# Chunk 0's key from half-scaled tokens, one-bank PSUM places and a new written order in an adaLN block with sliding attention and a token mixer

## The chip, the core and the metric

The kernel runs on one core of one Trainium2 chip. The metric is the time of one execution on the device in microseconds (us); before the change the median of three runs is 198.68 us (197.99 to 198.73). The core has five engines that run side by side, each working through its own instructions strictly in order: TensorE (PE, matmuls; PEld is its weight load), VectorE (DVE), ScalarE (ACT), GpSimd (POOL) and SyncE (SP), which here does nothing but issue DMAs. ScalarE also issues a few. Engines wait for each other by semaphores. SBUF is the memory that all engines work in; PSUM takes TensorE's results and has eight banks of 128 partitions by 512 float32.

## What is computed

One block on a sequence of 2048 tokens of width 512. Cut to what matters:

```
mod = silu(c) @ w_mod                      # six rows of 512: sa, ca, ga, sb, cb, gb
h = layernorm(x) * (1 + ca) + sa
q, k, v = h @ wqkv                         # 32 heads of 16
# each token attends to 8 tokens: itself, 2 back, 4 back ... 14 back
attn = softmax(q . k / 4, masked before token 0)
x = x + ga * ((attn @ v) @ wo)
h = layernorm(x) * (1 + cb) + sb
u = gelu(w1.T @ layernorm(h) + b1)         # mixes tokens: 2048 -> 1792 rows of 512
x = x + gb * (w2.T @ u + b2)               # 1792 -> 2048
```

Inputs and output are bfloat16.

## The kernel before

The 2048 tokens are cut into four chunks of 512 (`build_chunk(ch)`), each of four tiles of 128 tokens. A chunk goes through these named steps (the number behind the name is the chunk or the tile):

- `ln1s` takes the statistics of a tile, `rstd1` and `nb1` turn them into factors, and `ln1n` normalizes it into `n_sb`.
- `tr` transposes the chunk on TensorE into PSUM, as two halves `kp` of the width. `hT` evicts it into `hTb`, multiplied by `1 + ca` (`a1col`) and with `sa` (`sacol`) added, both as one value for each partition.
- `qkvq`, `qkvk`, `qkvv` are the matmuls, `evq`, `evk`, `evv` their evictions.
- `qk` multiplies q by eight shifted views of k on VectorE (4096 elements for each partition), `red` sums over the head on TensorE. `max`, `sub`, `exp`, `sum`, `rb`, `smul` are the softmax.
- `vd` are 16 DMAs that spread v into `vD`, shifted; `khalo` and `vhalo` bring the last 16 columns of the chunk before. `a2` and `a2ev` spread the weights, `pv` multiplies on VectorE, `pvacc` sums on TensorE, `oev` evicts.
- `wo` is the output projection, whose weights were multiplied by `ga` (`gmul`). `x1ev` evicts it and adds `x`: on VectorE in the eviction itself, on ScalarE by one more matmul with the identity (`on_pe`). `x1sq`, `rstd2`, `nb2`, `t`, `aff` are the second normalization, `ln3s`, `rstd3`, `nb3`, `h3` the third, which ends in `h3`.

Then the mixer: `mlp1_0` multiplies the first eight tiles of `h3` by blocks of `w1`, and its partial sums are parked in `gT` (`park`); `mlp1_1` does the other eight, `gadd` adds both, `gelu` and `gbm` follow; `mlp2` multiplies by `w2`, with `xb` and `fin` on VectorE and the store `st_out`.

What stands at the start: `c` and the first four tiles of `x` are loaded, then `wmodA` and `wmodB`, the halves (by rows) of `w_mod` for `sa` and `ca` together, 512 KB each, then the weights of k, x's next tiles and the weights of q. The silu of `c` is made from the exponential and logarithm (`silu_exp`, `silu_dve`); `modcols0` and `modcols1` compute `sa` and `ca` as columns with 16 one-column matmuls each, and `modcols_cp` evicts both. `warm0` to `warm4` are matmuls with the identity whose result nobody reads. For chunk 0 the transposes come in two halves of the tokens, but an `hT` eviction takes all 512 tokens of one width block. `build_mod_rows` computes the other four modulation rows (`modrows`, `mrow_ev`), and four DMAs (`bc0` to `bc3`) spread them over the partitions.

The order of all of it is written out: `ORDER` names every step, its engine where there is a choice (`:v` VectorE, `:a` ScalarE, `:g` GpSimd) and its place in PSUM (a number). `_Graph.schedule` checks that what a step needs stands ahead of it; then each engine gets its steps in that order, and one that waits holds up all behind it on its engine, DMA issues on SP included. PSUM is held as four tiles of two banks, and a step takes one of the four places, even where it needs one bank.

All instructions are recorded through one helper, so the profile names line 184 for nearly all, and they are told apart by the tiles they write and read.

Of the kernel before, what the change touches and what calls it, by code (L numbers as in the profile page):

```python
# [13 lines left out]
P = 128  # L14
# [13 lines left out]
consts ld_x00 consts2 ld_c warm0:0 ld_x02 ld_wmodA act_table ld_wmodB ld_w1a ld_x1a cps:1 warm1:2 ld_w1b silu_exp  # L28
ln1s0:v ld_x1b ln1s1:a ld_x2 ld_w0 silu_dve halo0 warm2:3 ln1s2:v rstd1_0_0 ln1s3:v modcols0:0 nb1_0_0:v ln1n0:v
warm3:1 rstd1_0_2 ln1n1:v nb1_0_2:v ln1n2:v modcols1 ln1n3:v tr0_00:2 tr0_10:3 modcols_cp:a tr0_02 tr0_12 hT0_0:a  # L30
warm4:1 hT0_1:v hT0_3:v qkvk0_0:0 hT0_2:v sc_rep ln1s7:v ln1s4:v ln1s9:v ln1s8:v ln1s11:v ln1s10:v qkvk0_1:1 qkvk0_2:3
qkvk0_0b qkvk0_1b ln1s5:a ln1s6:a rstd1_1_0 evk0_1:a nb1_1_0:g qkvq0_1:2 qkvq0_0:1 evk0_2:a evk0_0:a evq0_1:a ln1n7:a
# [5 lines left out]
exp0 qkvk1_2:0 modrows:2 tr2_10:3 sum0 evk1_2:a mrow_ev rb0 qk1_1 qk1_0 qk1_3 smul0 nb1_3_0:v qk1_2 tr2_00:0 qkvv1_0:2
a2_0:1 hT2_0:a hT2_1:a hT2_2:a ln1n12:a a2ev0:a evv1_0:a hT2_3:a ln1n15:a ln1n13:a ln1n14:a pv0_0 pv0_1 qkvv1_2:0
red1_0:1 red1_1 red1_2 red1_3 qkvq2_0:2 tr3_00:3 evv1_2:a evq2_0:a hT3_0:a bc0 khalo2 vd1_030 vd1_120 vd1_020 vd1_021  # L40
vd1_010 vd1_000 vd1_001 vd1_100 vd1_031 vd1_110 vd1_011 vd1_131 vd1_130 vd1_111 vd1_121 vd1_101 pvacc0_0:0 pvacc0_1
qkvk2_0:2 max1 pv0_3 pv0_2 oev0_1:a hT3_2:a sub1 tr3_10:0 qkvv2_0:3 evk2_0:a exp1 sum1 pvacc0_2:2 hT3_1:a rb1 hT3_3:a
gmul3:g gmul0:v gmul2:v gmul1:v qk2_1 smul1 qk2_0 pvacc0_3 qkvv2_2:1 oev0_3:a evv2_0:a evv2_2:a wo1:0 a2_1:2 x1ev1:a
a2ev1:a pv1_0 pv1_1 wo3:3 wo0:1 wo2:0 x1ev3:a x1sq1 x1sq3 x1ev0:a x1ev2:a qkvk2_2:2 pvacc1_0:3 qkvq2_2:1 pvacc1_1
x1sq2 evk2_2:a x1sq0 rstd2_0_0 evq2_2:a pv1_2 nb2_0_0:v pv1_3 t0:v qk2_3 qk2_2 qkvq3_0:0 pvacc1_2:2 pvacc1_3 qkvk3_0:1
t2:a t3:a oev1_1:a evq3_0:a oev1_3:a t1:a wo6:3 wo7:0 wo5:2 evk3_0:a x1ev6:a vhalo2 ld_b1 bc2 ld_w1_0_1 khalo3 bc1
vd2_101 ld_w1_0_2 vd2_000 ld_w1_0_0 vd2_131 vd2_121 vd2_010 vd2_001 vd2_030 vd2_031 ld_w1_0_3 vd2_020 red2_0:1 red2_1
wo4:3 x1sq6 x1ev7:a x1ev5:a x1sq7 x1sq5 x1ev4:a x1sq4 rstd2_1_0 red2_2 red2_3 aff0_0 qk3_1 ln3s0_1:v nb2_1_0:v
ln3s0_3:a max2 ln3s0_0:v ln3s0_2:v qkvv3_2:0 qkvk3_2:2 sub2 t4:a t7:g t6:g t5:g evv3_2:a exp2 rstd3_0_0 evk3_2:a
aff1_0 nb3_0_0:v qkvv3_0:3 biascols:0 sum2 qkvq3_2:2 rb2 h3_3:a evv3_0:a evq3_2:a ln3s1_2:a ln3s1_3:a h3_1:g h3_0:g  # L50
ln3s1_0:v biascols_cp ln3s1_1:v h3_2:v qk3_0 smul2 qk3_2 rstd3_1_0 mlp1_0_30_0:1 mlp1_0_31_0 mlp1_0_10_0:0 mlp1_0_11_0
a2_2:3 red3_0:2 red3_1 a2ev2:a nb3_1_0:v qk3_3 h3_6:a h3_4:a h3_5:a h3_7:v red3_2 mlp1_0_00_0:3 mlp1_0_01_0 red3_3
mlp1_0_00_4 mlp1_0_01_4 mlp1_0_10_4 mlp1_0_11_4 pv2_0 max3 park0_0:a sub3 pvacc2_0:3 vd2_120 vhalo3 ld_w1_0_6 vd2_011
ld_w1_0_4 vd3_030 vd2_110 vd2_021 vd2_100 vd2_130 vd3_001 vd2_111 vd3_031 vd3_000 vd3_011 vd3_110 vd3_020 vd3_010
# [160 lines left out]
def _tt1(n):  # L215
    return 0.08 + n / 960.0
# [764 lines left out]
```

## Time and profile before

| what | value |
|---|---|
| median of three runs | 198.68 us (197.99 to 198.73) |
| span of the profiled execution, first to last instruction | 197.0 us |
| time of the profiled execution beside its span | not listed by itself |
| granted TensorE clock, mean | 0.998 |
| busy: TensorE, VectorE, ScalarE, GpSimd | 190.1, 153.5, 123.4, 18.0 us |
| instructions | 3408 |
| read from HBM, written | 22.03 MB, 2.10 MB |

The span begins with the first instruction of any engine and ends with the last. A row of a timeline has the start and the length in us, the engine, the operation, the tiles written and read (buffer numbers left out), the shape and the count; idle time of the engine just before it stands in brackets, with what ended it. Neighbouring instructions of one kind are drawn together. A row of a table by stage gives the busy us of each engine in a stretch.

### The profile page before, as it was taken

How to read it: one execution, taken by the hardware profiler on the slowest of the kernel's cores; microseconds unless marked ns; L12 is line 12 of the kernel's file. 1: busy time of each engine (PE TensorE's matmuls, PEld its weight loads, DVE VectorE, ACT ScalarE, POOL GpSimd, SP SyncE). 2: the span in 40 equal slices, each digit the busy share in tenths (PEclk: the TensorE clock that was granted, in tenths of full speed). 3: DMA queues.
4: the chain of work that ended last, by engine and by line, in shares of the span. 5: the costliest groups of instructions: out<-in, count | busy, mean ns of one | idle time of the engine just before them, and what ended most of it. 6: DMA issues, size and time to landing. Idle time of an engine off the chain costs nothing.

```text
span 197.0 us, 3408 instructions
## 1 busy us (share of the span) xinstructions
PE 190.1 (97%) x1289; PEld 88.2 (45%) x1289; DVE 153.5 (78%) x198; ACT 123.4 (63%) x242; POOL 18.0 (9%) x46
## 2 busy tenths in 40 slices
PE   7889999999999999999999999999999999999994
PEld 2546545445443435433434444444444444444452
DVE  1699989999999999999999999928776127261463
ACT  5498999999999999993769999917541000000000
POOL 7003040090000004300000011000000000000000
PEclk9999999999999999999999999999999999999999
DMA  6999978507994994693999999990000871720112
GB/s 182 369 312 318 302 195 177 120 14 180 171 196 99 270 201 84 187 289 106 174 206 290 234 295 292 292 273 4 0 0 0 229 200 68 199 81 26 57 53 80
DMA packets 45348, 33.59 MB, mean 171 GB/s; under 512 B 5396, under 2 KB 42772, under 8 KB 45332
## 3 DMA queue, kind: packets, MB, share of 16 engines
q1 hardware_dynamic: 44908, 32.82, 67.2%
q10 hardware_dynamic: 424, 0.56, 1.0%
q8 instruction: 10, 0.16, 0.4%
q14 instruction: 6, 0.05, 0.1%
HBM read 22.03 MB, written 2.10 MB: 122 GB/s over the span
## 4 chain that ended last, share of the span: by engine, by line
PE 64%; DVE 12%; DMA 11%; ACT 5%; SPq 3%; issue 2%; ACTq 0%; DVEq 0%
PE ps L184 64%; DMA vD<-v_c 5%; DMA w_q<-in_A_wqkv_dram 4%; SPq L184 3%; DVE pvb L184 3%; DVE prod L184 3%; DMA vD<-in_w_mod_dram 3%; DVE st L184 2%; ACT n_sb L184 1%; DVE h L184 1%; ACT hTb L184 1%; DVE gT L184 1%; ACT v_c L184 1%; DVE ee L184 1%; DVE nm L184 1%
## 5 line engine op out<-in xcount | busy, mean ns | idle before, releaser
L184 DVE TENSOR_TENSOR pvb<-a2sb,vD 128x4096 bf16<-128x4096 bf16 x16 | 36.0, 2284 | 0.2 <-issue 0.2
L184 PE MATMUL ps<-h,wst 128*128 128x512 bf16 x128 | 29.5, 379 | 0.0
L184 DVE TENSOR_TENSOR prod<-q_sb,k_c 128x4096 bf16<-128x4096 bf16 x9 | 20.4, 2285 | 0.1
L184 PEld LDWEIGHTS <-wst 128*128 128x128 bf16 x128 | 12.1, 98 | 16.0 <-issue 1.7
L184 PE MATMUL ps<-gT,vD 128*128 128x512 bf16 x84 | 19.1, 379 | 0.0
L184 PE MATMUL ps<-hTb,w_q 128*128 128x512 bf16 x64 | 15.1, 381 | 1.0 <-DMA w_q<-in_A_wqkv_dram 0.7
L184 DVE TENSOR_TENSOR q_sb<-ps,q_sb 128x512 bf16<-128x512 f32 x8 | 5.4, 687 | 13.6 <-PE ps L184 13.6
L184 PE MATMUL ps<-woq,o_sb 128*128 128x512 bf16 x64 | 15.8, 379 | 0.0
L184 PEld LDWEIGHTS <-w_q 128*128 128x128 bf16 x96 | 9.9, 109 | 12.6 <-issue 2.5
L184 PE MATMUL ps<-hTb,w_v 128*128 128x512 bf16 x64 | 15.0, 380 | 0.0
L184 PE MATMUL ps<-hTb,w_k 128*128 128x512 bf16 x64 | 15.0, 380 | 0.0
L184 DVE TENSOR_TENSOR k_c<-ps,k_c 128x512 bf16<-128x512 f32 (+2 forms) x9 | 5.6, 629 | 11.7 <-PE ps L184 11.7
L184 PEld LDWEIGHTS <-o_sb 128*128 128x128 bf16 x106 | 9.7, 98 | 10.5 <-issue 0.4
L184 PEld LDWEIGHTS <-vD 128*128 128x128 bf16 x116 | 9.2, 97 | 11.4 <-DMA vD<-in_w_mod_dram 1.5
L184 PE MATMUL ps<-gT,pvb 128*128 128x512 bf16 x56 | 12.9, 379 | 0.0
L184 PEld LDWEIGHTS <-w_k 128*128 128x128 bf16 x80 | 8.7, 111 | 8.9 <-issue 0.8
L184 PE MATMUL ps<-gT,prod 128*128 128x512 bf16 x56 | 12.2, 379 | 0.0
L184 PEld LDWEIGHTS <-w_v 128*128 128x128 bf16 x80 | 8.3, 111 | 8.2 <-issue 1.3
L184 ACT ACTIVATE junk<-xx,su 128x512 bf16<-128x512 bf16 x16 | 11.5, 720 | 0.5 <-DVE xx L184 0.2
L184 DVE BATCH_NORM_STATS2 st<-xx 128x6 f32<-128x512 bf16 x11 | 7.4, 671 | 4.7 <-DMA xx<-in_A_x_dram 4.7
L184 ACT ACTIVATE hTb<-ps,sacol,a1col 128x512 bf16<-128x512 bf16 x13 | 9.6, 782 | 0.5 <-PE ps L184 0.5
L184 DVE TENSOR_TENSOR gT<-q_sb,k_c 128x4096 bf16<-128x4096 bf16 x4 | 9.1, 2284 | 0.0
(113 smaller groups left out, 315.1 us busy)
## 6 DMA issues: line engine op xcount, KB each, us to landing
vD<-v_c SPq DMA_DIRECT2D x64, 131.5 KB, 4.6
wst<-in_B_w_dram SPq DMA_DIRECT2D x8, 512.0 KB, 6.1
vD<-in_B_w_dram SPq DMA_DIRECT2D x3, 896.0 KB, 7.3
wst<-in_w_mod_dram SPq DMA_DIRECT2D x4, 512.0 KB, 9.3
prod<-in_B_w_dram SPq DMA_DIRECT2D x2, 896.0 KB, 11.0
pvb<-in_B_w_dram SPq DMA_DIRECT2D x2, 896.0 KB, 8.1
xx<-in_A_x_dram SPq DMA_DIRECT2D x4, 256.0 KB, 4.7
xx<-in_A_x_dram SPq DMA_DIRECT2D x2, 512.0 KB, 7.7
```

Source lines behind the costliest of these rows:

```text
L184: r = fn(*a, **k)
```

## The change

- **Loads at the start.** The first two tiles of `x` come as two DMAs of 128 KB (`ld_x00`, `ld_x01`). Of the two modulation blocks the scale (`ca`) comes first, as two DMAs of 256 KB (`ld_ca0` on ScalarE's queue, `ld_ca1` on SP's), then both halves of k's weights, and only then the shift (`ld_sa`, 512 KB). The weights of q come ahead of `x2`.
- **Column sums.** `colsa` computes the scale's columns over all of the depth in 16 matmuls, `a1_cp` evicts it; `colss` does the shift's, and `sa_cp` evicts it twice, as float32 and as bfloat16 (`sabf`).
- **Chunk 0's key.** The transposed tokens are evicted in halves of 256 tokens (`hk0_0` to `hk3_2`, eight steps), multiplied by the scale alone, into four unused rows of `gT`. The key is computed from these, 32 matmuls of 256 columns (`qkvk0_j_0`, `qkvk0_j_2`) in place of 16 of 512. What the shift adds to the key is one value for each row of k: `kbias` computes it with 16 one-column matmuls of k's weights and `sabf`, and `evk0` adds it as the bias at the eviction, in four steps of one bank each. `hadd0` to `hadd3` add the shift to the scaled tokens for chunk 0's q and v.
- **PSUM.** There are eight places of one bank. A step that needs two banks takes two neighbouring places; transposes, the one-bank parts of chunk 0, `wo`, `mlp2` and the small sums take one. The tiles remain four of two banks. Chunk 0's key holds four places at once. `biascols` writes both of its results into one bank.
- **Order.** `ORDER` is new throughout. On GpSimd there are now `ln1n1`, 5, 4, 11, 8, 10, 9, 13 and 14, all four `gmul`, `t3`, 1, 2, 0, 6, 4 and 15, `h3_1`, 2, 9, 8 and 13, and five of the `nb` steps (before: `ln1n6`, 4, 10, 11, 8, `gmul3`, `t7`, 6, 5, `h3_1`, 0, 8 and two `nb`). `x1ev` is on ScalarE for 14 of 16 tiles (before 9). `bc0` is issued ahead of three of chunk 0's `vd` DMAs.

The core of the diff:

```diff
-consts ld_x00 consts2 ld_c warm0:0 ld_x02 ld_wmodA act_table ld_wmodB ld_w1a ld_x1a cps:1 warm1:2 ld_w1b silu_exp
...
+consts ld_c ld_x00 ld_x01 ld_ca0 ld_ca1 ld_x02 act_table ln1s1:v ld_wk0 ln1s0:a warm4:0 ld_wk2 rstd1_0_0 consts2
+warm0:0 cps:0 silu_exp warm1:1 silu_dve nb1_0_0:v ln1n0:v warm2:1 ln1s2:v ln1s3:a ld_sa colsa:0 rstd1_0_2 ln1n1:g
+warm3:1 halo0 a1_cp:v tr0_10:1 hk1_0:v nb1_0_2:v tr0_00:0 ln1n2:v ln1n3:v hk3_0:v ld_x1b hk0_0:a hk2_0:a ld_x1a tr0_02
+ld_wq tr0_12 ld_b1 hk1_2:v hk0_2:a ld_x2 qkvk0_2_0:2 colss:3 ld_b2 hk3_2:v hk2_2:a ld_wv sa_cp:a hadd3:a ln1s4:a ld_x3
+ln1s7:v qkvk0_0_0:4 qkvk0_3_0:5 qkvk0_1_0:3 kbias:0 qkvk0_0_2 ln1s6:v hadd2:v ln1s5:v ld_wo2 hadd0:a hadd1:v qkvk0_1_2
+qkvk0_3_2 qkvk0_2_2 qkvq0_1:1 qkvq0_2:6 rstd1_1_0 kb_cp:v sc_rep evk0_3:v nb1_1_0:v qkvq0_0:0 ln1n6:v ln1n7:v ln1s10:v
...
+qkvq1_0:2 qkvk1_0:0 red0_0:4 red0_1 red0_2 ld_wmod2 ld_wo1 red0_3 evv0_2:a rstd1_2_0 evq1_0:a ln1s15:a evk1_0:a
+ln1s14:a ln1s12:a ln1s13:v khalo1 vd0_101 qkvq1_2:6 vd0_131 vd0_030 vd0_011 max0 ld_wo3 nb1_2_0:g vd0_031 ln1n11:g
+sub0 ln1n8:g vd0_000 vd0_111 ld_wo0 vd0_021 exp0 vd0_010 ln1n10:g rstd1_3_0 evq1_2:a ln1n9:g qkvk1_2:2 sum0 tr2_10:0
+nb1_3_0:g rb0 tr2_00:1 evk1_2:a hT2_1:a modrows:6 qkvv1_2:4 mrow_ev hT2_3:a hT2_0:a qk1_1 vd0_100 vd0_110 vd0_130
+vd0_020 hT2_2:a bc0 gmul2:g vd0_001 gmul0:g qk1_0 smul0 a2_0:2 qk1_2 qk1_3 qkvv1_0:6 gmul1:g qkvk2_0:0 a2ev0:a
+evv1_0:a gmul3:g red1_0:2 vd0_120 vhalo1 vd0_121 ld_w1_0_0 ln1n13:g ln1n14:g evv1_2:a pv0_0 evk2_0:a ln1n12:a khalo2
...
-    NPS = 4
-    ps = [psp.tile([P, 2, 512], F32, name=f"ps{i}") for i in range(NPS)]
+    NPS = 8
+    ps = [psp.tile([P, 2, 512], F32, name=f"ps{i}") for i in range(NPS // 2)]
...
     def bank(s_, h):
-        return ps[s_.i][:, h, :]
+        return ps[s_.i // 2][:, s_.i % 2 + h, :]
...
+    def f_kb():
+        for j in range(4):
+            for kt in range(KT):
+                nc.tensor.matmul(bank(sl_kb, 0)[:, j:j + 1], lhsT=_ap(w_p[1][:, kt, j:j + 1], [[4, P]]),
+                                 rhs=sabf[:, kt:kt + 1], start=(kt == 0), stop=(kt == KT - 1), skip_group_check=True)
...
+                if ch == 0:
+                    dst = hraw[:, kt, t0:t1]
+                    alts = [("act", _act(n_, 1), lambda dst=dst, src=src, sc_=sc_: nc.scalar.activation(
+                                dst, src(), ACT.Identity, scale=sc_)),
+                            ("dve", 0.32, lambda dst=dst, src=src, sc_=sc_: nc.vector.tensor_scalar(
+                                dst, src(), sc_, None, op0=ALU.mult))]
...
+            for (g0, g1) in parts:
+                for j in range(4):
+                    def f(j=j, g0=g0, g1=g1):
+                        for kt in range(KT):
+                            nc.tensor.matmul(bank(sk[j], 0)[:, g0 * P:g1 * P], lhsT=_ap(w_p[1][:, kt, j:j + 1], [[4, P]]),
+                                             rhs=hraw[:, kt, g0 * P:g1 * P], start=(kt == 0), stop=(kt == KT - 1))
```

More of the change, by code (lines that the diff above doesn't have):

```diff
@@ L27 @@
 ORDER = """
-consts ld_x00 consts2 ld_c warm0:0 ld_x02 ld_wmodA act_table ld_wmodB ld_w1a ld_x1a cps:1 warm1:2 ld_w1b silu_exp
[L29 to L32, printed above, removed]
@@ L38 @@
[L38 to L42, printed above, removed]
@@ new lines, with f_sa_dve @@
+    mod_cols(1, range(KT), "colsa")
+    G.add_any([("act", 0.2, lambda: nc.scalar.activation(a1col[:], bank(sl_m[1], 0)[:, 0:KT], ACT.Identity, bias=1.0)),
+               ("dve", 0.1, lambda: nc.vector.tensor_scalar(a1col[:], bank(sl_m[1], 0)[:, 0:KT], 1.0, None, op0=ALU.add))],
+              reads=[sl_m[1]], writes=["a1col"], name="a1_cp", lat=0.1, use=[sl_m[1]])
+    mod_cols(0, range(KT), "colss")
+    def f_sa_dve():
+        nc.vector.tensor_copy(sabf[:], bank(sl_m[0], 0)[:, 0:KT])
+        nc.vector.tensor_copy(sacol[:], bank(sl_m[0], 0)[:, 0:KT])
```

282 lines of the change are left out of this document (161 added, 121 removed).

## The prediction

> **What bounds the kernel now.** I read the page's busy times first, then the chain that ended last in order of time, then the timeline of each engine over the opening, and last the rows of VectorE and GpSimd side by side.
>
> ```profile
> PE 190.1 (97%) x1289; PEld 88.2 (45%) x1289; DVE 153.5 (78%) x198; ACT 123.4 (63%) x242; POOL 18.0 (9%) x46
> ```
>
> From the chain of waits, three columns: start, us, what:
>
> ```profile
> 1.38 5.32 DMA vD<-in_w_mod_dram
> ...
> 6.71 7.94 DMA w_q<-in_A_wqkv_dram
> ...
> 14.70 19.33 PE ps L184 x145
> ...
> 86.30 106.59 PE ps L184 x585
> ```
>
> TensorE looks full, but a matmul's modelled end overlaps the next one, so small waits hide in "busy". The timeline of TensorE tells more:
>
> ```profile
> 1.41 1.89 PE L184 MATMUL ps<-ident 128*128 128x512 bf16 x4 [1.41 <-POOL onecol L184]
> ...
> 8.23 0.54 PE L184 MATMUL ps<-sc,vD 128*128 128x1 bf16 x16
> 8.64 1.05 PE L184 MATMUL ps<-ident,n_sb 128*128 128x128 bf16 x16
> ...
> 10.40 3.61 PE L184 MATMUL ps<-hTb,w_k 128*128 128x512 bf16 x16
> 14.70 3.65 PE L184 MATMUL ps<-hTb,w_q 128*128 128x512 bf16 x16 [0.69 <-DMA w_q<-in_A_wqkv_dram]
> ...
> 36.58 0.42 PE L184 MATMUL ps<-ee,selB 64*32 64x128 bf16 x32 [0.39 <-DVE ee L184]
> ...
> 192.71 1.38 PE L184 MATMUL ps<-gT,o_sb 128*128 128x512 bf16 x16
> ```
>
> Sixteen matmuls of 512 columns take 3.61, and one alone 0.38 (the groups' mean is 379 to 381 ns): the step from one to the next is (3.61 - 0.38)/15 = 0.2155. After 10.40 the code issues 785 such units: 192 for q, k and v, 64 for `wo` and 9 identity matmuls beside them, 224 each for `mlp1` and `mlp2`, 8 for `sub`, and 64 for `red` and `pvacc` (four quarter-width ones run as one). 785 x 0.2155 = 169.2. Transposes and `sum` (80 at 0.056), `a2` (4 x 0.35) and `modrows` (16 of quarter width, 0.9) add 6.8: 176.0. From 10.40 to the last end, 192.71 + 1.38 = 194.1, pass 183.7, so TensorE loses 7.7 us in waits. The span is 10.4 + 176.0 + 7.7 + 2.9 (last eviction, store) = 197.0.
>
> Where the 7.7 go, a table by stage says (the stretch and its length, then busy us of TensorE, its weight loads, VectorE, ScalarE and GpSimd, the granted clock, the DMA share, GB/s):
>
> ```profile
> 30.00:50.00 20.00, 19.52 (x213) 10.36 (x212) 20.00 (x15) 19.32 (x31) 5.25 (x1) 1.00 0.54 121
> 50.00:70.00 20.00, 19.99 (x156) 8.63 (x155) 19.97 (x13) 19.84 (x40) 0.00 (x0) 1.00 0.90 187
> 70.00:86.30 16.30, 15.62 (x137) 7.28 (x130) 16.09 (x25) 15.95 (x40) 3.78 (x5) 1.00 0.78 177
> ```
>
> From 30 to 86 VectorE has no time left (56.06 of 56.30), and TensorE is fed at its pace; after 86.3 TensorE alone counts. So three things set the time: when q starts, what VectorE has to carry until 86, and TensorE's own work behind that.
>
> **The opening.** The change needs 0.5 MB of modulation weights before the first eviction where before 1 MB was awaited; the two waits named above for `vD` and `w_q` are what it aims at. I follow the new order by the old rows.
>
> ```profile
> 1.78 0.47 SPq L184 DMA_DIRECT2D vD<-in_w_mod_dram  x1
> 1.83 1.28 ACT L184 ACT_TABLE_LOAD   x1 [1.83 <-issue]
> 4.00 0.61 ACT L184 ACTIVATE junk<-xx 128x512 bf16<-128x512 bf16 x1
> 5.46 0.46 ACT L184 ACTIVATE lv<-mv,epscol 128x1 f32<-128x1 f32 x2
> 5.95 0.20 ACT L184 ACTIVATE rs<-lv 128x2 f32<-128x2 f32 x1
> 9.81 1.45 DVE L184 TENSOR_SCALAR hTb<-ps,a1col,sacol 128x512 bf16<-128x512 bf16 x3 [1.10 <-PE ps L184]
> 11.30 0.69 DVE L184 BATCH_NORM_STATS2 st<-xx 128x6 f32<-128x512 bf16 x1
> 16.67 4.49 DVE L184 TENSOR_TENSOR prod<-q_sb,k_c 128x4096 bf16<-128x4096 bf16 x2
> ```
>
> In the rows above, the table load ends at 3.1, so ScalarE takes `ln1s0` from 3.15 to 4.6 (1.46 by the rows 4.00 to 5.46), `rstd1_0_0` to 5.3 (0.69) and `silu_exp`, now behind both, to 5.95. Both column sums and the normalized tiles wait for that: GpSimd has `ln1n1` by 7.1. But TensorE comes later: its first eight warming matmuls stand ahead of `cps`, at some 0.43 each (row 1.41: four in 1.89, less the overlap of the last, an estimate), to 4.8; then eight more at 0.2155, `colsa` and five more, with the wait for the weights between, to 8.2. The transposes run from 8.2. `hk1_0` follows half a microsecond behind the first of them (before: the last transpose at 8.64 + 15 x 0.055 = 9.47, its eviction at 9.81), VectorE does `ln1n2` and `ln1n3` ahead of `hk3_0`, which ends at 10.0. `tr0_02` and `tr0_12` stand in front of the first key matmul and need the halves' readers out of the bank: first key matmul at 10.4, as before.
>
> The key block is the same 32 x 256 columns, 3.5 us (no row has such a matmul; the ends are the 0.055 of a 128-column transpose and a full step's 0.2155, and I take half a step, 0.108, as a quarter of the columns went at a quarter of it with a new load each), and now holds `colss` and `kbias`, 32 one-column matmuls at 25 ns (row 8.23), 0.8. So q can start at 14.8. `hadd0` on ScalarE, behind `sa_cp`, `hadd3` and `ln1s4`, ends at 14.65 by the same sums. Before, q started at 14.70, held by its weights. In the new order the q weights have `x2` behind them instead of ahead (0.5 MB less in their queue), and I take them as landed. Splitting `ld_x00` costs one more SP issue, some 0.47, ahead of `x02`, hidden behind `ln1s0`. For the opening I take **+0.2**, between -0.9 (if the warming matmuls don't hold up the transposes) and +1.0 (a key block at a full step would be +3.4, which the transposes' row speaks against; +1.0 comes if the `hk` or `hadd` steps slip by a stats step, some 0.8: row 11.30 and its short second step). VectorE's first product moves from 16.67 to some 17.6: it takes `evk0_3`, `hadd` and three stats first, but has one stats step fewer between the products and `max0`.
>
> **The move of work.** Fourteen, not nine, `x1ev` evictions are on ScalarE; each brings one identity matmul (`on_pe`), all five added ones behind 86: 5 x 0.2155 = **+1.1** on TensorE, which has no gap there. VectorE's list from its first product to `qk3_3` is shorter by 0.3 (three `gmul`, `t0` and small ones go, three `h3` and `t5` come), and ScalarE's gets four norms fewer. All of that goes to GpSimd, from 11 normalizations and one `gmul` to 21 and four. This is what the sum hangs on, so the rows of GpSimd beside VectorE's:
>
> ```profile
> 14.28 0.20 POOL L184 TENSOR_TENSOR nb<-mv,rs 128x4 f32<-128x4 f32 x1 [9.34 <-ACT rs L184]
> 14.58 0.23 POOL L184 TENSOR_SCALAR nb<-nb 128x4 f32<-128x4 f32 x1
> 25.90 2.27 POOL L184 TENSOR_SCALAR n_sb<-xx,rs,nb 128x512 bf16<-128x512 bf16 x3 [9.48 <-DVE nb L184]
> 38.97 5.25 POOL L184 TENSOR_TENSOR woq<-woq,ga_bc 128x512 bf16<-128x512 bf16 x1 [10.80 <-DMA ga_bc<-mrow]
> 117.95 0.77 POOL L184 TENSOR_SCALAR h<-h,rs,nb 128x512 bf16<-128x512 bf16 x1
> ```
>
> ```profile
> 38.72 4.49 DVE L184 TENSOR_TENSOR pvb<-a2sb,vD 128x4096 bf16<-128x4096 bf16 x2
> 43.13 1.22 DVE L184 TENSOR_REDUCE nm<-ps 128x128 bf16<-128x1024 f32 x1
> 118.19 0.99 DVE L184 TENSOR_SCALAR h<-h,mv,rs 128x512 bf16<-128x512 bf16 x2
> ...
> 120.11 0.73 DVE L184 TENSOR_SCALAR h<-xx,rs,nb 128x512 bf16<-128x512 bf16 x2
> ```
>
> The one `gmul` on GpSimd took 5.25 us: it lay beside two products of VectorE and ended at 44.22, 1.09 after the second gave way to a reduction out of PSUM. And at 118.19 two normalizations of VectorE took 0.99 where the same pair took 0.73 at 120.11 (0.26 lost) while GpSimd held out to 118.72. The two engines exclude each other; the normalizations at 25.90 took 0.76 each because VectorE was at stats and a reduction. The Trainium skill, page "SBUF — State Buffer", section "Who interferes with whom", states this: a VectorE instruction with two SBUF inputs and a GpSimd one that reads SBUF share a port pair, and the one that starts first blocks the other for the whole instruction. By that rule GpSimd would have got in between the two products, at 40.92; the trace says it did not, so I count port time and leave open who waits.
>
> From 27 to 86 the new order gives GpSimd 14 normalizations (0.76), four `gmul` (1.09) and four `nb` pairs (0.6, from 14.28 until the next step at 14.9): 17.4 us. VectorE leaves it free in six stats steps (0.8), three reductions (1.1, row 43.13 less its overlap) and about 1 us of waits: 9.1. So 8.3 us must be taken from products or waited out. Who pays: `tr2` on TensorE needs `ln1n8` to `ln1n11`, `tr3` needs `ln1n13` and `ln1n14` (which stand behind all four `gmul`, and these behind `bc0`), `aff0` needs `t0` to `t3`; behind each stands all of TensorE's or VectorE's queue. Least is nothing, most all 8.3. The nearest row is 118.19, where a normalization of 0.77 cost VectorE 0.26, a third: a third of 8.3 is 2.8, and I take **+2.8**.
>
> `bc0` also moves on SP's queue ahead of the last `vd0` copies, so `pv0_1` waits for `modrows` and `mrow_ev`. I put that inside the ends of the term above: while VectorE waits for them the port is free.
>
> **Banks and order.** Eight one-bank places where four two-bank ones stood let transposes, `wo` and `mlp2` hold half as much, and `mlp1_0` pieces stand earlier in the new order to fill TensorE's waits. The most that can be won is the 7.7. The waits the profile names for TensorE in the middle, 0.39, 0.31 and 0.37, sum to 1.1; I take **-1.0**, ends 0 and -5. The tail is the same by the rows (14 and the last 128 columns of 15 last, their stores behind): 0. `biascols`, two copies, the `hk` evictions (eight of half size for four): under `ln1s` work, 0; without that cover 0.3 each.
>
> **Sum.** +0.2 + 1.1 + 2.8 - 1.0 = +3.1 on a span of 197.0: 200.1. The profile gives the profiled execution's span alone; the middle of the runs, 198.68, is 1.7 above it. So 201.8.
>
> **The rivals.** *Faster:* the places and fillers win back most of TensorE's waits (-5), and GpSimd's work falls into VectorE's free stretches. +0.2 + 1.1 - 5 = -3.7: 195.0. For it: before, GpSimd's eleven normalizations all found such stretches. It decides once the fillers win more than 1.3 plus what the port costs. *Slower still:* VectorE's strings of products keep the port as at 38.97. Then two of `ln1n8` to `ln1n11` pass before `max0` ends at 29.5, and the last waits for `qk1_1` and `qk1_0` (2.2 each, to 34) or also for `smul0`, `qk1_2` and `qk1_3` (to 39.8); TensorE, done with `sum0` at 33, stands at `tr2` for 2 to 7 us. It stands again at `tr3`, where VectorE's `smul1` in turn needs `sum1` from behind `tr3`. That is the whole 8.3 in place of 2.8: 207.3. *Nothing:* the port costs nothing that matters, and the order wins the 1.1 back: 198.9. *A release after each product:* a GpSimd step waits 2.2 at most, and VectorE then pays the whole 0.76 for each of eight steps that fall on products: 6.1 in place of 2.8, 205.1. The row at 38.97 speaks against it. It is the reading of the Trainium skill's page "SBUF — State Buffer", same section.
>
> **How the numbers follow.** Forecast (200 to 204) 0.42; slower still 0.18; a release after each product 0.05; nothing 0.10; faster 0.25. A measurement here can't tell less than 0.5%, 1 us, from no change. Faster 0.25, same 0.10, slower 0.65. The range leaves out a tenth on each side: 195.0 to 206.5; the likeliest case alone has 200 to 204.
>
> **What would show it.** First key matmul at 10.4 and first q at 14.8 (within 0.6). GpSimd steps of over 1.5 us beside VectorE products, or products of over 2.5; a wait of TensorE at `tr2` or `tr3` named GpSimd or `n_sb`. Five more identity matmuls on `xx`. It is wrong if q starts before 14, or if GpSimd's normalizations stay at 0.77 and products at 2.28 throughout, or if TensorE's losses after 10.4 fall under 6.

## The result and the profile after

| | before | after |
|---|---|---|
| median | 198.68 us (197.99 to 200.11, 5 runs) | 229.83 us (228.70 to 233.38, 5 runs) |
| ratio | 1 | 1.154, 95% interval 1.147 to 1.161 |
| forecast | | 201.8, range 195.0 to 206.5 |

The change costs some 30 us where 3 were forecast. Two of the five runs after, the profiled one of 232.47 us among them, lie over 1.5% above the fastest, so the ratio above and the differences below go by the other three, whose median is 229.0 us, and the rows are read for where time is lost, not for the total.

From the page, the busy times:

```profile
PE 200.4 (87%) x1326; PEld 93.2 (40%) x1326; DVE 153.9 (67%) x189; ACT 125.4 (54%) x257; POOL 45.7 (20%) x65
```

VectorE and ScalarE do what they did before (153.9 and 125.4 against 153.5 and 123.4), but TensorE now covers 87% of its span instead of 97%, and it is busy 10 us longer with nearly the same matmuls. The waits are visible in the timeline of TensorE (start, length, then in brackets how long it stood idle just before and what ended that):

```profile
6.28 1.86 PE L188 MATMUL ps<-ident 128*128 128x512 bf16 x4 [1.16 <-ACT ecol L188]
8.47 1.86 PE L188 MATMUL ps<-ident 128*128 128x512 bf16 x4 [0.33 <-DVE sc L188]
...
13.93 0.38 PE L188 MATMUL ps<-ident,n_sb 128*128 128x128 bf16 x4 [0.44 <-DVE gT L188]
15.70 0.69 PE L188 MATMUL ps<-ident,n_sb 128*128 128x128 bf16 x8 [1.39 <-ACT gT L188]
16.19 1.06 PE L188 MATMUL ps<-gT,w_k 128*128 128x256 bf16 x4
...
22.06 2.10 PE L188 MATMUL ps<-hTb,w_q 128*128 128x512 bf16 x9
...
63.36 0.29 PE L188 MATMUL ps<-ident,n_sb 128*128 128x128 bf16 x1 [6.29 <-POOL n_sb L188]
```

The first key matmul starts at 16.19 (before 10.40), q at 22.06 (before 14.70). The strange rows are the first two. `warm1` and `warm2` multiply the identity by itself, read nothing that was computed, and yet wait for `ecol`, the silu of `c`, and for `sc`. VectorE's side of the same stretch:

```profile
8.25 0.16 DVE L188 TENSOR_TENSOR sc<-ps,ecol 128x4 bf16<-128x4 f32 x1 [2.65 <-PE ps L188]
...
12.89 0.16 DVE L188 TENSOR_SCALAR a1col<-ps 128x4 f32<-128x4 f32 x1 [3.26 <-PE ps L188]
...
23.12 0.16 DVE L188 COPY kbcol<-ps 128x4 f32<-128x4 f32 x1 [2.46 <-PE ps L188]
```

`sc` reads place 0, whose one matmul ended at 5.1, and `ecol`, which is ready by 6.7; it waits until 8.25, when `warm1` in place 1 is done. `a1col` reads place 0 and waits for `warm3` in place 1; `kbcol` reads place 0 and waits for q's block in place 1. In each pair the two places are the two banks of one PSUM tile. The change cut the places in half but left the tiles at two banks, and the program's waits go by tile.

The second loss is GpSimd's. From its timeline and from VectorE's:

```profile
49.88 10.64 POOL L188 TENSOR_TENSOR woq<-woq,ga_bc 128x512 bf16<-128x512 bf16 x4 [5.54 <-DMA vD<-v_c]
60.50 3.56 POOL L188 TENSOR_SCALAR n_sb<-xx,rs,nb 128x512 bf16<-128x512 bf16 x2
```

```profile
49.79 5.45 DVE L188 TENSOR_TENSOR pvb<-a2sb,vD 128x4096 bf16<-128x4096 bf16 x2
55.16 1.21 DVE L188 TENSOR_REDUCE nm<-ps 128x128 bf16<-128x1024 f32 x1
56.29 6.37 DVE L188 TENSOR_TENSOR pvb<-a2sb,vD 128x4096 bf16<-128x4096 bf16 x2
```

Four scalings took 10.64 us, and the pairs of products beside them 5.45 and 6.37 where such a pair took 4.49 before. `ln1n13` and `ln1n14` stand behind the scalings, and `tr3` on TensorE waits 6.29 us for them (the last TensorE row above).

A third loss is TensorE's clock. Two rows of a table by stage (stretch and length, busy us of TensorE, its weight loads, VectorE, ScalarE and GpSimd, granted clock, DMA share, GB/s):

```profile
10.00:20.00 10.00, 7.91 (x77) 5.19 (x76) 4.29 (x13) 3.81 (x12) 0.00 (x0) 0.83 1.11 326
60.00:70.00 10.00, 6.17 (x33) 3.09 (x34) 3.58 (x3) 2.31 (x5) 4.06 (x3) 0.66 0.92 156
```

In finer stretches the clock is at 0.50 from 16.1 to 19.5, nearly all of the first half of the key block, and from 60.5 to 67.3, and at 1.00 elsewhere before the last matmul. TensorE works for some 6.9 us of these; at half the clock that is by estimate 3.4 us lost. Before the change the clock stays at 1.00 until the last matmul.

### The profile page after: what moved, and what is told of

Read it like the earlier page. It is cut to its first block, busy times and chain, and to the rows that moved or that the text cites. A ratio compares the mean times of both kernels' runs of the same rounds, so it can differ in the third digit from the quotient of the medians.

```text
span 230.8 us, 3508 instructions
## 1 busy us (share of the span) xinstructions
PE 200.4 (87%) x1326; PEld 93.2 (40%) x1326; DVE 153.9 (67%) x189; ACT 125.4 (54%) x257; POOL 45.7 (20%) x65
## 4 chain that ended last, share of the span: by engine, by line
PE 49%; ACT 28%; DVE 8%; POOL 6%; issue 4%; DMA 3%; SPq 0%; DVEq 0%; ACTq 0%
PE ps L188 49%; ACT junk L188 9%; POOL woq L188 3%; ACT xx L188 3%; DVE h L188 3%; ACT v_c L188 3%; ACT q_sb L188 2%; ACT lv L188 2%; ACT hTb L188 2%; DVE q_sb L188 2%; DVE st L188 2%; ACT o_sb L188 2%; POOL n_sb L188 2%; DMA xx<-in_A_x_dram 1%; ACT k_c L188 1%
## 5 line engine op out<-in xcount | busy, mean ns | idle before, releaser
L188 DVE TENSOR_TENSOR pvb<-a2sb,vD 128x4096 bf16<-128x4096 bf16 x16 | 38.7, 2462 | 3.5 <-PE ps L188 2.2
L188 PE MATMUL ps<-woq,o_sb 128*128 128x512 bf16 x64 | 16.3, 379 | 3.3 <-ACT xx L188 2.3
L188 POOL TENSOR_SCALAR n_sb<-xx,rs,nb 128x512 bf16<-128x512 bf16 x9 | 13.3, 1490 | 18.7 <-DVE nb L188 14.8
L188 PE MATMUL ps<-hTb,w_v 128*128 128x512 bf16 x64 | 16.5, 404 | 0.2 <-ACT q_sb L188 0.2
L188 PE MATMUL ps<-ident,n_sb 128*128 128x128 bf16 x64 | 5.7, 230 | 10.6 <-POOL n_sb L188 7.8
L188 PEld LDWEIGHTS <-w_k 128*128 128x128 bf16 x112 | 11.3, 116 | 8.2 <-issue 1.2
L188 POOL TENSOR_SCALAR h<-h,rs,nb 128x512 bf16<-128x512 bf16 x5 | 4.7, 946 | 48.8 <-DVE nb L188 48.8
L188 PEld LDWEIGHTS <-ident 128*128 128x128 bf16 (+1 forms) x77 | 7.1, 108 | 13.9 <-issue 9.2
L188 ACT ACTIVATE hTb<-ps,sacol,a1col 128x512 bf16<-128x512 bf16 x12 | 8.9, 784 | 6.4 <-PE ps L188 6.4
```

The source lines that it names most:

```text
L188: r = fn(*a, **k)
```

## The experiments

The theories: **A**, neighbouring places of one PSUM tile wait for each other; **B** (B1 in its sharper form), GpSimd and VectorE keep each other out (the port of the prediction), and strings of products make it dear; **C**, a rival of both: the new loads and the new order are late by themselves. D, E and F came up on the way and are explained where they appear. All ratios are against the kernel before on the same chip.

**apart.** Only place numbers differ from the changed kernel, 86 of them, beginning so:

```diff
-warm1:1 warm2:1 colsa:0 warm3:1 tr0_10:1 colss:3 qkvk0_0_0:4 qkvk0_3_0:5 qkvk0_1_0:3 kbias:0
+warm1:2 warm2:2 colsa:2 warm3:4 tr0_10:4 colss:6 qkvk0_0_0:3 qkvk0_3_0:4 qkvk0_1_0:0 kbias:5
```

> The changed kernel with its order, engines and loads untouched; only place numbers differ, so that one-bank steps that are alive together stand in different two-bank tiles where there is room (12 waits between neighbours of one tile are left in the program, of 39). Theory A (neighbours in one tile wait for each other): the first key matmul starts at 10.4 to 12 us instead of 16.19, q at 15 to 18 instead of 22.06, the whole 7 to 14 us shorter than the changed kernel, 214 to 222. Theory B (the shared port of GpSimd and VectorE is the whole loss): the opening moves but the end stays above 226. Rival C (the new loads and the new order themselves are late): first key matmul stays at 15 to 16 us, total 227 to 231.

222.72 us (ratio 1.124, 1.121 to 1.126): 6.3 shorter than the changed kernel's 229.0 (6.0 by the two ratios), a little less than the 7 to 14 that A said. Its TensorE timeline:

```profile
10.73 0.60 PE L188 MATMUL ps<-gT,w_k 128*128 128x256 bf16 x4
...
15.17 3.62 PE L188 MATMUL ps<-hTb,w_q 128*128 128x512 bf16 x16
...
55.02 0.29 PE L188 MATMUL ps<-ident,n_sb 128*128 128x128 bf16 x1 [6.28 <-POOL n_sb L188]
...
56.38 3.62 PE L188 MATMUL ps<-hTb,w_v 128*128 128x512 bf16 x8
...
60.65 1.92 PE L188 MATMUL ps<-hTb,w_v 128*128 128x512 bf16 x8
```

The key starts at 10.73 and q at 15.17, nearly as before the change: C is wrong for the opening's start. The GpSimd wait of 6.28 stays, and behind it eight matmuls take 3.62 that take 1.92 four microseconds later: here the clock is at 0.50 from 50.4 to 60.7 (see apart_gm_warm).

**before_pairs.** The same theory from the other side: the kernel before with nothing changed but how PSUM is declared.

```diff
-    ps = [psp.tile([P, 2, 512], F32, name=f"ps{i}") for i in range(NPS)]
+    quad = [psp.tile([P, 4, 512], F32, name=f"ps{i}") for i in range(NPS // 2)]
+    ps = [quad[i // 2][:, 2 * (i % 2):2 * (i % 2) + 2, :] for i in range(NPS)]
```

> The kernel before, its order, places and engines untouched; only the PSUM tiles are declared twice as large, so that places 0 and 1 lie in one tile of four banks and places 2 and 3 in another. No address, instruction or order differs. Theory A: steps in neighbouring places now wait for each other, the time rises by 10 to 50 us, to 209 to 250, and new waits of VectorE and ScalarE on PE named ps appear. If waits go by bank and not by tile: 198 to 200, no change.

274.97 us (1.384, 1.374 to 1.394): 76 us for a declaration, more than A's 50. From its table of waits (us in total, times, longest):

```profile
PE ps L184 <- ACT ee L184: 10.3, 3, 8.1
PE ps L184 <- ACT a2sb L184: 8.2, 4, 3.9
DVE xx L184 <- PE ps L184: 8.5, 2, 6.5
```

TensorE waits for evictions it has nothing to do with, and VectorE for matmuls whose result it does not read. The chip does not ask for this, since the kernel before runs the same instructions in 198.5 us without these waits; the program does. The Trainium skill, page "PSUM — Partial Sum Buffer", section "PSUM bank collisions raise a hardware error", asks to guard PSUM by bank and quadrant, two readers included; by that rule no two banks need a wait, and here the waits go wider than it. No run here shows what happens on one bank without a wait.

**pool_back and apart_pool_back.** Sixteen steps that the change had put on GpSimd go back, in the new order (but the three scalings stand later in it), once with the changed kernel's places and once with those of apart.

```diff
-ln1n5:g nb1_2_0:g ln1n9:g nb1_3_0:g gmul2:g gmul0:g gmul1:g ln1n13:g ln1n14:g nb2_0_0:g t3:g t1:g t2:g t0:g nb2_1_0:g t4:g
+ln1n5:v nb1_2_0:v ln1n9:a nb1_3_0:v ln1n13:a ln1n14:a gmul2:v gmul0:v gmul1:v nb2_0_0:v t3:a t1:a t2:a t0:v nb2_1_0:v t4:a
```

> The changed kernel with 16 steps that it had moved to GpSimd put back on the engines they had before (three scalings of the output weights, four of the norms n_sb, five of the t norms, four of the small means); places as in the changed kernel. Theory B: the idle TensorE before tr2 and tr3 that is named after n_sb of GpSimd (8.0 us together) falls under 2, the n_sb steps take 0.8 us each or under 1.5, pairs of pvb products take 4.5 to 4.7 us instead of 5.45 and 6.37; total 8 to 14 us shorter, 214 to 220. Theory A as the whole loss: within 2 us of the changed kernel, 226 to 231.

> Both edits. If A and B are both right and add up: 200 to 210. If they overlap (one only uncovers the other): no better than the better of the two alone by more than 3 us. If C is right: above 222.

233.99 us (1.178, 1.173 to 1.184) and 222.16 (1.121, 1.116 to 1.126): pool_back is some 5 longer than the changed kernel, apart_pool_back no shorter than apart. Taken alone that speaks against B, but the waits of apart_pool_back show that the edit brought its own:

```profile
DVE nb L188 <- ACT rs L188: 17.0, 7, 7.7
...
PE ps L188 <- DVE nm L188: 5.1, 1, 5.1
```

The waits for `n_sb` ahead of `tr3` are gone, as B said, but the small means `nb2`, now on VectorE at the place where GpSimd had them, make VectorE stand 7.7 us for ScalarE's `rs`, and TensorE then stands for `nm`. The edit took out one wait and put in another. So the next one leaves the second half of the list where it is.

**apart_gm, apart_gm_max, apart_gm_max_x1.** On top of apart: only the three scalings (again later in the order) and four norms of the first layer go back; then also `max2` ahead of the steps that wait for GpSimd's t norms (theory **D**: the place of that reduction costs TensorE 3.8 us); then also five `x1ev` back on VectorE.

```diff
-ln1n5:g ln1n9:g gmul2:g gmul0:g gmul1:g ln1n13:g ln1n14:g
+ln1n5:v ln1n9:a ln1n13:a ln1n14:a gmul2:v gmul0:v gmul1:v
-aff0_0 red2_2 ln3s0_2:v red2_3 qkvv3_0 ln3s0_3:v qk3_1 ln3s0_0:v max2 ln3s0_1:a
+red2_2 red2_3 max2 aff0_0 ln3s0_2:v ln3s0_3:v ln3s0_0:v ln3s0_1:a qkvv3_0 qk3_1
-x1ev9:a x1ev10:a x1ev11:a x1ev14:a x1ev15:a
+x1ev9:v x1ev10:v x1ev11:v x1ev14:v x1ev15:v
```

> The kernel apart with three scalings of the output weights, ln1n5 and the norms ln1n9, ln1n13 and ln1n14 back on VectorE and ScalarE; the t norms and small means stay on GpSimd, other than in pool_back. Theory B1 (strings of VectorE products keep GpSimd out, and tr3 pays for it): the 6.3 us in which TensorE waits for n_sb ahead of tr3 and the slow matmuls behind it go, the first matmul with the output weights starts at 57 to 59 us instead of 66.0; total 212 to 215 against 222.7. If apart_pool_back showed no gain because GpSimd's work costs nothing: 221 to 224.

> apart_gm with chunk 2's max (VectorE) moved in the order ahead of chunk 0's affine step and its statistics and of the product qk3_1, no engine changed. Theory D (the new order puts VectorE's reduction behind steps that wait for GpSimd's t norms, and TensorE waits 3.8 us for nm at 88 to 92): that wait falls under 1 us, total 3 to 7 us below apart_gm, 206 to 211. If the place in the order does not matter: within 1 us of apart_gm.

> apart_gm_max with the evictions x1ev 9, 10, 11, 14 and 15 back on VectorE, so five identity matmuls fewer. By the prediction's term 0.4 to 1.1 us shorter than apart_gm_max; if ScalarE's queue between 120 and 150 us is what holds TensorE there, 2 to 4 us shorter; if VectorE is the fuller engine there, longer.

apart_gm took 216.35 us (1.089, 1.083 to 1.095), 6.4 below apart, somewhat less than B said. The other two took 217.28 (1.093, 1.083 to 1.103) and 218.11 (1.096, 1.088 to 1.104): D falls, and the five identity matmuls of the prediction cannot be seen. Why D falls is one row of TensorE in each. First apart_gm, then apart_gm_max:

```profile
85.35 1.01 PE L188 MATMUL ps<-nm,ident 128*128 128x512 bf16 x2 [4.19 <-DVE nm L188]
```

```profile
86.48 3.57 PE L188 MATMUL ps<-hTb,w_k 128*128 128x512 bf16 x8 [4.88 <-ACT v_c L188]
```

With the reduction moved ahead, `nm` is in time, and now ScalarE's eviction `v_c` is late, since a statistics step that waits for `aff0` stands ahead of it on ScalarE. At this place both engines have steps in line behind one chain (t norms on GpSimd, `aff0` on VectorE), and TensorE is out of other work. Moving one step only changes the name of the wait.

**before_gmul.** B in the kernel before, alone:

```diff
-gmul0:v gmul2:v gmul1:v
+gmul0:g gmul2:g gmul1:g
```

> The kernel before with the three scalings of the output weights moved from VectorE to GpSimd, behind the one that is there already; nothing else differs. Theory B1: the four scalings run from 39.0 to 52 to 56 us (3 to 5 us each beside the products), and the first matmul with the output weights waits for the last: 52.5 to 56 instead of 51.69; total 199.5 to 204. If the port does not matter: four scalings of 1.0 us, 197 to 199.

200.25 us (1.008, 1.005 to 1.012): by the ratio 1.7 longer, inside what B1 said. The group of scalings on GpSimd (ns: shortest, median, longest; start of first and last):

```profile
L184 POOL TENSOR_TENSOR woq<-woq,ga_bc x4: 1150/3204/3971, 43.4 to 51.6; 128x512 bf16<-128x512 bf16 x4
```

The one that falls on VectorE's reduction takes 1.15, the median beside products 3.2. No engine is named as waiting for the scalings; what grows is VectorE's pair of products beside them, 6.40 us in place of 4.49.

**open_only and open_places.** The changed kernel's opening, 89 steps, and behind it the kernel before: its order, engines and places. (open_only also has chunk 0's statistics and norms on the old engines.) The two kernels differ in eleven place numbers of the opening, those of apart and those of the changed kernel:

```diff
-warm1:2 warm2:2 colsa:2 warm3:4 tr0_10:4 colss:6 qkvk0_0_0:3 qkvk0_3_0:4 qkvk0_1_0:0 kbias:5 qkvq0_0:4
+warm1:1 warm2:1 colsa:0 warm3:1 tr0_10:1 colss:3 qkvk0_0_0:4 qkvk0_3_0:5 qkvk0_1_0:3 kbias:0 qkvq0_0:0
```

> The changed kernel's opening (its first 89 steps: scale block first, key from scaled tokens in halves, shift as bias) with the places of apart, and behind it the order, engines and places of the kernel before (each place there as a tile of its own). Theory E (what is left after the false waits and the port is the new order behind the opening): 197 to 201, TensorE's first key matmul 10 to 11 us, q at 14.7 to 15.5. If the opening itself, its loads or its longer bias path costs: 203 to 212. If the opening gains: below 197.

> open_only with one difference: the opening's place numbers are those of the changed kernel, so 15 waits between neighbouring places are in the program instead of 3. Theory A: first key matmul at 15 to 16.5 us and q at 20.5 to 22.5 as in the changed kernel, and the time 5 to 8 us above open_only. If the late loads and not the places made the changed kernel's opening late: same as open_only within 1 us.

202.00 us (1.021, 1.018 to 1.024) and 208.82 (1.057, 1.052 to 1.061): the eleven numbers alone cost 6.8, as A said. open_only itself is above what E said, and its q is late. TensorE in open_only, then in open_places:

```profile
11.08 0.60 PE L188 MATMUL ps<-gT,w_k 128*128 128x256 bf16 x4
...
16.81 3.61 PE L188 MATMUL ps<-hTb,w_q 128*128 128x512 bf16 x16 [1.14 <-ACT hTb L188]
```

```profile
6.99 1.86 PE L188 MATMUL ps<-ident 128*128 128x512 bf16 x4 [1.87 <-ACT ecol L188]
...
14.98 0.61 PE L188 MATMUL ps<-ident,n_sb 128*128 128x128 bf16 x8 [1.39 <-ACT gT L188]
...
22.06 2.10 PE L188 MATMUL ps<-hTb,w_q 128*128 128x512 bf16 x9 [1.55 <-ACT hTb L188]
```

The same waits as in the changed kernel come back with the numbers, and q is at 22.06 to the hundredth.

**open_only2, open_eng, apart_eng.** open_only2 has chunk 0's steps on the changed kernel's engines; with it the order and the places of the opening are the same in all four cells of a table of order against engines (57 steps have other engines; six of them, `ln1s4` to `ln1s6`, `ln1n6`, `ln1n7` and `nb1_1_0`, belong to chunk 1 but stand inside the opening). The order brings its places with it: by the expectations' counts the new one still has 12 waits between neighbours of one tile, the opening alone 3. Theory **E**: the order carries what is left.

```diff
-ln1s1:a ln1s0:v ln1s3:v ln1n1:v
+ln1s1:v ln1s0:a ln1s3:a ln1n1:g
```

> The changed kernel's opening, now with chunk 0's own statistics and norms on the engines of the changed kernel (open_only had put them back), places apart, and behind it order, engines and places of the kernel before. Theory E (the opening alone costs next to nothing, the order behind it and its engines cost the rest): q at 15.0 to 15.6, 198.5 to 201. If the opening costs by itself as in open_only: 201.5 to 203.

> open_only2 with the 57 steps behind the opening put on the engines of the changed kernel, their places in the old order kept. If the engines carry the rest (GpSimd's added work and the longer way of the t norms): 212 to 222. If the new order carries it: 200 to 206.

> The other cell: apart with the same 57 steps on the engines of the kernel before, in the new order (the three scalings of the output weights stand later, where VectorE has the gate row). If the new order carries the rest: 214 to 222. If the engines carry it: 199 to 207. If order and engines only fit each other: above 218, worse than apart_gm.

| behind the opening | old engines | new engines |
|---|---|---|
| old order | open_only2 201.62 (1.016, 1.011 to 1.020) | open_eng 215.28 (1.083, 1.076 to 1.089) |
| new order | apart_eng 229.62 (1.158, 1.151 to 1.165) | apart 222.72 (1.124, 1.121 to 1.126) |

E falls as it was put: neither order nor engines carry it alone. The new engines cost 13.7 in the old order and save 6.9 in the new one; the new order costs 28.0 with the old engines and 7.4 with the new. The two were written for each other, and together they are still 21.1 worse than the old pair. Part of the price of the new order is the clock: its mean in the profiled executions is 0.999 and 1.000 in the two cells of the old order, 0.970 and 0.969 in those of the new. In apart TensorE works some 8 us at half clock, by estimate 4 of the 7.4. The opening with old order and old engines costs 3.5. Rows of open_only2, of TensorE, VectorE and ScalarE:

```profile
15.74 3.61 PE L188 MATMUL ps<-hTb,w_q 128*128 128x512 bf16 x15 [1.14 <-ACT hTb L188]
```

```profile
19.67 4.49 DVE L188 TENSOR_TENSOR prod<-q_sb,k_c 128x4096 bf16<-128x4096 bf16 x2 [0.82 <-ACT q_sb L188]
```

```profile
13.50 0.63 ACT L188 ACTIVATE junk<-xx 128x512 bf16<-128x512 bf16 x1
...
14.98 0.71 ACT L188 ACTIVATE hTb<-gT,sacol 128x512 bf16<-128x512 bf16 x1
```

q waits for the added pass that puts the shift on the scaled tokens (`hadd`, on ScalarE), 1.0 later than before, and the first product starts 3.0 later. But ahead of that pass ScalarE does a second statistics step, 13.50 to 14.98, that the old engines put there (`ln1s5`); the change has it on VectorE. With the change's engines q has no such wait:

```profile
14.97 3.62 PE L188 MATMUL ps<-hTb,w_q 128*128 128x512 bf16 x15
```

That is open_eng; open_rest, which has the six, starts q at 14.93 without the wait, open_pool, which has not, at 16.33 with it. In apart q starts at 15.17, and the first product starts at 18.73 (open_eng) and 18.14 (apart), 2.1 and 1.5 later than before. So the 3.5 is the price of the new opening with old engines inside it, and most of q's lateness in it is not the change's.

**apart_gm_warm.** Theory **F**: a long wait of TensorE is paid twice, the second time as a lowered clock. Twelve identity matmuls whose result nobody reads go into the wait for `nm`:

```diff
-    WARM=(4, 4, 4, 5, 4),
+    WARM=(4, 4, 4, 5, 4, 12),
-qkvv3_0:2 ln3s0_3:v
+qkvv3_0:2 warm5:5 ln3s0_3:v
```

> apart_gm with 12 identity matmuls more, into a place of their own, behind chunk 3's second value block, where TensorE otherwise waits 4.2 us for nm. They take 2.6 us of that wait. Theory F (an idle stretch of TensorE of some 3 us halves its granted clock for the next 3 to 4 us): the granted clock stays at 1.00 after the wait, the eight key matmuls behind it take 1.9 us and not 2.85, total 0.5 to 2 us below apart_gm's 216.35. If the slow matmuls there come from elsewhere: no shorter, or longer by what does not fit into the wait.

215.16 us (1.084, 1.078 to 1.090) against 216.35: 1.2 shorter, though the intervals overlap, so the total does not decide. What settles the clock are the tables by stage (stretch and length, busy us of TensorE, its weight loads, VectorE, ScalarE and GpSimd, granted clock, DMA share, GB/s) and TensorE's rows, first of apart_gm, then of apart_gm_warm:

```profile
83.00:85.30 2.30, 0.00 (x0) 0.00 (x0) 2.27 (x5) 1.06 (x5) 0.00 (x0) 0.93 0.00 0
85.30:87.30 2.00, 1.95 (x5) 0.69 (x5) 1.83 (x3) 1.63 (x2) 0.00 (x0) 0.50 0.08 34
87.30:89.30 2.00, 2.00 (x8) 0.87 (x7) 2.00 (x5) 0.23 (x2) 0.89 (x1) 0.72 0.28 105
```

```profile
86.16 3.00 PE L188 MATMUL ps<-hTb,w_k 128*128 128x512 bf16 x8
```

```profile
81.63 2.75 PE L188 MATMUL ps<-ident 128*128 128x512 bf16 x12
86.65 0.59 PE L188 MATMUL ps<-nm,ident 128*128 128x512 bf16 x2 [2.27 <-DVE nm L188]
87.08 1.89 PE L188 MATMUL ps<-hTb,w_k 128*128 128x512 bf16 x8
```

```profile
85.30:87.30 2.00, 0.65 (x4) 0.32 (x4) 1.87 (x4) 1.76 (x6) 0.00 (x0) 1.00 0.00 0
87.30:89.30 2.00, 2.00 (x11) 1.08 (x10) 1.97 (x2) 1.30 (x3) 0.00 (x0) 1.00 0.22 86
```

Without the filler the clock falls to 0.50 at the end of the 4.2 us wait and stays there until about 88.4 (0.72 over a stretch of 2.0 means 1.1 at half), and the eight key matmuls take 3.00. With it the wait is 2.3, the clock stays at 1.00 and they take 1.89. For the clock F holds. What it is worth to the whole kernel is not shown: `nm` came 1.3 later in the execution with the filler, because VectorE was that late already before the filler, and q's matmuls behind start at 88.81 against 88.99.

**open_pool and open_rest.** The 57 engines of open_eng in two parts: the 21 steps that moved onto GpSimd (the 16 below and five `nb`), and the other 36, of which 30 change between VectorE and ScalarE and six leave GpSimd.

```diff
-gmul0:v gmul1:v gmul2:v ln1n5:v ln1n9:a ln1n13:a ln1n14:a t0:v t1:a t2:a t3:a t4:a t15:v h3_2:v h3_9:v h3_13:v
+gmul0:g gmul1:g gmul2:g ln1n5:g ln1n9:g ln1n13:g ln1n14:g t0:g t1:g t2:g t3:g t4:g t15:g h3_2:g h3_9:g h3_13:g
```

> open_only2 with only the 21 steps that the change had moved onto GpSimd put there, in the old order. Theory B1 (port): a norm or a scaling that falls beside products takes 2 to 5 us instead of 0.8 to 1.0, TensorE waits ahead of tr3 and of the first mlp blocks; 208 to 214 against 201.6, most of open_eng's 215.3. If the port is not the cause: 201 to 204.

> open_only2 with the other 36 of the 57 steps on their new engines (VectorE and ScalarE exchange work), GpSimd as before. Under B1 the smaller part: 202 to 207. If the exchange between VectorE and ScalarE costs most: 208 to 214.

207.93 us (1.046, 1.040 to 1.051) and 210.41 (1.058, 1.054 to 1.063): 6.3 and 8.8 above open_only2. GpSimd's part is a little below what B1 said and less than half of open_eng's 13.7, where B1 said most; the exchange between VectorE and ScalarE (with the six), expected to be the smaller part, is the larger. GpSimd in open_pool, and VectorE beside it:

```profile
37.09 2.13 POOL L188 TENSOR_SCALAR nb<-nb 128x4 f32<-128x4 f32 x1
...
39.32 5.30 POOL L188 TENSOR_SCALAR n_sb<-xx,rs,nb 128x512 bf16<-128x512 bf16 x1
...
47.38 8.59 POOL L188 TENSOR_TENSOR woq<-woq,ga_bc 128x512 bf16<-128x512 bf16 x4
```

```profile
36.87 2.28 DVE L188 TENSOR_TENSOR h<-q_sb,k_c 128x4096 bf16<-128x4096 bf16 x1
39.07 0.68 DVE L188 TENSOR_TENSOR ee<-ee,rb 128x1024 bf16<-128x1024 bf16 x1
39.67 2.28 DVE L188 TENSOR_TENSOR gT<-q_sb,k_c 128x4096 bf16<-128x4096 bf16 x1
41.87 4.89 DVE L188 TENSOR_TENSOR pvb<-a2sb,vD 128x4096 bf16<-128x4096 bf16 x2
```

A step of four elements for each partition took 2.13, beside a product of 2.28 that had started 0.22 before it (0.23 in the prediction's row without one), and a norm of 0.77 took 5.30. In open_rest no single wait stands out. These rows of TensorE are its two longest behind 86:

```profile
120.70 0.61 PE L188 MATMUL ps<-pvb,stack 128*32 128x512 bf16 x8 [1.27 <-DVE pvb L188]
...
139.40 6.08 PE L188 MATMUL ps<-h,wst 128*128 128x512 bf16 x26 [1.28 <-DVE h L188]
```

Which of the 36 steps cost most was not separated.

## Why the prediction was wrong, step by step

The 30.9 us between 229.0 and 198.06 (the kernel before beside open_only2) divide, by undoing one cause after the other, as: false waits between neighbouring places 6.3 (changed kernel to apart), GpSimd's added work on the first layer's norms and the scalings 6.4 (apart to apart_gm), the rest of the new order and its engines 14.7 (apart_gm to open_only2), the opening with old engines 3.6 (open_only2 to before). By the ratios, each against the kernel before on its own chip, the four are 6.0, 6.9, 14.5 and 3.1. That is one way down; the cells above show that order and engines do not simply add up. The first two parts have a cause that the runs show. Of the 14.7, by estimate 3 are the clock (in apart_gm it is at half from 37.2 to 40.6 and from 85.0 to 88.4, with TensorE at work for 6.5 us of it); what makes the rest stays open.

- **"Banks and order", -1.0 (0 to -5): the step that failed.** It took eight places for eight, read from the place numbers that eight independent steps were possible, and costed nothing for what shares a tile. The diff that the prediction quotes has the answer in it: `NPS // 2` tiles, and `bank` taking `s_.i // 2`. The sign was wrong, +6.3 for the places alone (6.8 in open_places), and its bounds excluded a loss without a reason. The same step took the new order as at worst neutral; with the engines that go with it, it is the largest part, 14.7, and only its size is shown, not which steps of the order cost it.
- **Exchange between VectorE and ScalarE, costed at nothing** but for five identity matmuls ("VectorE's list from its first product to `qk3_3` is shorter by 0.3"). In the old order it cost 8.8, with the six steps that leave GpSimd. From 30 to 86 the prediction's own table had VectorE at 56.06 of 56.30 and ScalarE full too; there the sum of a list says little if, as is argued here and not shown, what counts is whether each step is there when TensorE needs it.
- **The opening, +0.2 (-0.9 to +1.0).** With the places apart the followed order came out: first key matmul 10.73 (forecast 10.4), q 15.17 (14.8, within 0.6), sixteen half-width key matmuls in 1.91 (0.11 each, as taken), first product 18.14 (17.6). In the changed kernel neither holds, 16.19 and 22.06, by the false waits and the half clock behind them. The 3.5 in front of the old kernel is above the upper end, but by a statistics step ahead of `hadd0` that the change does not have there; the prediction named just that slip for its upper end (+1.0), and q is 1.0 later. What the opening costs with its own engines and an order that suits them, no run shows.
- **The port, +2.8 (0 to 8.3).** The mechanism was right and the places were, too: TensorE stands at `tr3`, named `n_sb`, for 6.29. The term measured 6.4 in the new order (seven of the steps) and 6.3 in the old one (all 21). The mistake was the nearest row: a norm that cost VectorE 0.26 stood beside another short norm, while the added work fell beside products of 2.28. The rivals were nearer in the term: "slower still" with 8.3, and "a release after each product" with 6.1. The second, given 0.05, is what the four scalings did in the changed kernel, where three of them take 3.2 and each product pays some 0.94; what the first says, a hold over a string, shows in the norm of 5.30. Their 207.3 and 205.1 still missed the total.
- **Five identity matmuls, +1.1.** Not seen: taking them back, which also puts five evictions on VectorE, gave 218.1 against 217.3, inside the intervals.
- **What no term covered.** Waits of TensorE lower the clock behind them. In the changed kernel that happens twice, by estimate 3.4 us together; in the one place tried, eight matmuls fell from 3.00 to 1.89.
- **The rivals.** All were wrong in the total. "Faster" needed the fillers to win back waits that the places had in truth added. The signs named for B (GpSimd steps over 1.5, products over 2.5, a wait at `tr3`) all appeared; that q starts late was listed only as "within 0.6".

No kernel here beats the one before. The nearest that keeps the change's idea, open_only2, is 1.6% slower, and what the idea aimed at, an earlier first key matmul, does not come about either: with the places apart it starts at 10.00 to 11.32 in the kernels here (10.40 before), and q at 14.70 at the earliest (14.70 before).

## What to carry to other kernels

When a buffer is cut into more places, look at what the program's waits go by: the places must be tiles of their own, or steps that are alive together must lie in different tiles; a wait of a step for something that it does not read is the sign in the trace. Work moved to GpSimd is priced by the VectorE instruction that runs beside it, not by its own length. An order written for one set of engines is not neutral with another: here the swap cost 13.7 one way and 28.0 the other. And before a wait of TensorE is accepted in a sum, add what the clock does behind it.

## What the runs showed of the hardware that was not expected

- **GpSimd and VectorE: held over one product or two, and turns.** Some GpSimd steps that meet a string of VectorE instructions are held over several of them (5.30 us over a scaling, two products and part of a third in open_pool). Others get in after one product, and then the two take turns: from 49.88 to 60.50 in the changed kernel four scalings take 10.64 between them, three of them some 3.2 each, while a pair of products grows from 4.49 to 6.37, so each product pays some 0.94. The Trainium skill, page "SBUF — State Buffer", section "Who interferes with whom", has whichever starts first hold the ports for one instruction. The turns agree with that, and the wait over several products does not; the measured row decides. Why one step is held over two and another over one, no run settles.
- **TensorE's clock.** In apart_gm it fell to half 3.8 us after the last matmul (0.93 mean over 83.0 to 85.3, so 0.3 us at half) and came back some 3 us after matmuls resumed. The Trainium skill, page "TensorE: Matmul & The Clock Gate", section "What's actually happening", gives about 3.4 us for both; this place agrees roughly. There the wait of 4.2 us cost over 5, and the one of 2.3 in apart_gm_warm only itself. But the length of one wait does not decide: in the changed kernel the clock is at half from 16.1 to 19.5 behind waits of 0.25, 0.44 and 1.39 us with only transposes between them, and in apart_gm from 37.2 to 40.6 behind one of 1.80. What is the same in these traces is the length at half: 3.4 us in these three places, 6.8 from 60.5 to 67.3 in the changed kernel, 10.2 from 50.4 to 60.7 in apart, each once, twice or three times 3.4.
- **False waits between readers.** These belong to the program and not to the chip. Two readers waited for each other too: in before_pairs VectorE's copy `b1col`, out of place 0, is held until ScalarE's `lns` has read another place (2.9 us, of which 0.9 after its own matmuls had ended). In all, 11 place numbers were worth 6.8 us; declared sizes of tiles alone were worth 76.
